# Sliding-window attention feeding a two-layer MLP: memsets and q spreading leave GpSimd, and q of three batches comes in 64-value rows

## The chip, the cores and the metric

The kernel runs on one core of a Trainium2 chip. Its time is device time in microseconds (us) of that core for one execution; lower is better. Before the change it takes 315.79 us, the median of 3 runs (315.48 to 317.68).

## The reference

```python
def _attn_ref(q, k, v):                       # each (8, 8, 576, 64): batch, head, position, dim
    scores = (1.0 / np.sqrt(64)) * np.matmul(q, k.transpose(0, 1, 3, 2))
    rel = pos[:, None] - pos[None, :]
    scores = np.where((rel >= 0) & (rel < 64), scores, -1e9)
    attn = softmax(scores)                    # over the keys
    return np.matmul(attn, v)
x = attn_out.transpose(0, 2, 1, 3).reshape(4608, 512)
h = x @ w_in                                  # 512 -> 2048
out = (h - np.tanh(h)) @ w_out                # 2048 -> 512, float32 (4608, 512)
```

A query sees itself and the 63 keys before it.

## The kernel before, in words

Everything is computed in bfloat16 and added up in float32. Two pieces of work run beside each other: attention of 8 batches, and an MLP over 9 chunks of 512 tokens. A chunk can start when the attention of the batches that its tokens lie in has been normalised and transposed.

**Attention.** A batch has 4 pairs of heads, so that pairs are numbered 0 to 31 (`g`), and 9 windows of 64 queries. For each window the scores of 64 queries of both heads against 128 keys are one matmul (three windows at a time, `Rp`, line 300), the exponential is ScalarE's (`Rx`, line 305), a multiply with a mask is VectorE's (`M`, line 393), and two pairs at a time are multiplied with v (`PP`, line 418) and normalised (`DR`, `DN`, lines 426 to 438). The result is transposed into the chunk's tile by TensorE in the early batches (`Xp`) and by a DMA transpose in the later ones (`Y`, line 472).

**Where v comes from.** v is loaded in rows of 64 values into two tiles `vw` that alternate by batch (`LV`, line 160). Two VectorE copies of 64 partitions by 2080 values then put the other half of each window in place (`Z`, `cross_rows`, lines 166 and 167).

**Where k and q come from.** k of batches 3 to 7 is loaded in rows of 64 values (`lr`, line 176) and turned by a DMA transpose into `kw` (`tk`, line 181). q takes two roads. In batches 3 to 5 (`LQ`, `load_all`, line 114) a batch's q is loaded in runs of 384 values, cast from the loaded tile to a tile of the pair (`cq`, `cast`, line 88 on ScalarE or 90 on VectorE), transposed by TensorE (`Ep`, line 261) and copied from PSUM into `qT` (`Ea`, `Eb`). In batches 6 and 7 GpSimd spreads the two heads of a pair over the halves of a zeroed tile `qz` (`cz`, `cast_q`, line 128, two copies a pair), the tile is written to DRAM (`bo`, line 133) and read back by a DMA transpose into `qT` (`td`, line 138). There are two `qz`, which alternate by pair: a spreading into one waits until the write of two pairs before has left it. The zeros in `qz` (`z`, line 235) and the pads of `kw` (`mk`, line 220) are written once, by GpSimd.

**MLP.** `H` is a tile of the first layer (four matmuls of 512 columns, line 487), `A` its tanh on ScalarE (line 495), `G` the subtraction on VectorE (line 501), `W` four matmuls of the second layer (line 526), and `O` a copy out of PSUM on ScalarE or VectorE with the store on SyncE's DMA queue (line 542).

**Order.** Nothing is scheduled at run time. `PLAN` is a list of words such as `H.3.11` or `cz.25`, written out in full; `play` issues them one after the other, and each engine executes its own instructions in that order. A word with `.a` or `.v` runs on ScalarE or VectorE. Loads (`lk`, `lq`, `LQ`, `LV`, `lr`, `wi`, `wo`) are issued by GpSimd in its own order with its other instructions. Words that issue DMAs from SyncE (`tk`, `bo`, `td`, `Y`, and the store of `O`) stand in SyncE's order.

Of the kernel before, what the change touches and what calls it, by code (L numbers as in the profile page):

```python
# [15 lines left out]
def kernel(  # L16
# [9 lines left out]
    nc = tc.nc  # L26
    B, H, S, D = q.shape
# [58 lines left out]
    def move(eng, o, i):  # L86
        if eng is nc.scalar:
            nc.scalar.activation(o, i, ACT.Copy)  # L88
        else:
            eng.tensor_copy(o, i)  # L90
# [20 lines left out]
    def load_all(b, n):  # L111

        t = rows_all[n][b % 2][0:P]
        nc.gpsimd.dma_start(out=t, in_=(q if n == "q" else k)[b].rearrange("h (p e) d -> p h (e d)", e=E))
        for pr in range(NP):
            stage[b * NP + pr, n] = t[:, pr::NP]
# [7 lines left out]
    def cast_q(g):  # L124

        i = stage.pop((g, "q")).rearrange("p h (e d) -> p h e d", d=D)
        for h in range(2):
            nc.gpsimd.tensor_copy(qz[g % 2][:, h, :, 64 * h:64 * h + 64], i[:, h])  # L128
# [89 lines left out]
    def pads_kw():  # L218
        for i in range(2):
            nc.gpsimd.memset(kw[i][:, :, 0:64], 0.0)  # L220
# [13 lines left out]
    def more_zeros(i):  # L234
        nc.gpsimd.memset(qz[i], 0.0)
# [318 lines left out]
    def subtract(c, m, s=None):  # L554
# [6 lines left out]
        LK=lambda b: load_all(b, "k"), LQ=lambda b: load_all(b, "q"),  # L561
# [14 lines left out]
    def play(script):  # L576
# [5 lines left out]
        mt.0 mv.0 mt.1 lk.3.p lq.0.s lk.1.p u ck.1.a lq.1.p LV.0.1 cq.0.a lk.0.s i mv.1 U.11 cq.1.v mq.1 U.1  # L582
        LV.0.3 Ep.1.3 Fp.1.2 Ec.1.3.v lq.3.p ck.0.v U.4 U.1.3 h Fc.1.2.a LV.0.2 Fp.0.2 LV.0.0 LV.0.4 Rp.1.1.4
        lk.2.p Ep.0.3 Ec.0.3.v lq.2.p Fc.0.2.a Rx.1.1.4 Rp.1.0.0 Rp.0.1.4 Rx.1.0.0 Fp.3.2 Ep.3.3 Rx.0.1.4
        Rp.0.0.0 Fc.3.2.v Z.0 Ec.3.3.a Rx.0.0.0 U.4 lk.5.p lk.7.p lq.5.p lk.6.p n Rp.3.1.4 P.0 Fp.2.2 D.0 Ep.2.3
        Rp.3.0.0 Fc.2.2.a lq.4.p lk.4.p Ec.2.3.v lq.7.p U.2 ck.5.v Rx.3.0.0 P.1 Rx.3.1.4 Fp.5.3 cq.5.v Rp.2.0.0
        Fc.5.3.a Rp.2.1.4 Rx.2.0.0 D.1 Rx.2.1.4 Ep.5.3 Xp.0.0.1.2 lv.1.1.1 P.3 wi.0 Eb.5.3.v wi.1 ck.4.v
        Ea.5.3.a wi.2 Xc.0.0.1.2.a Fp.4.3 Fc.4.3.a Rp.5.0.4 lv.1.1.0 lq.6.p D.3 lt.1 cq.4.v P.2 Rx.5.0.4
        lv.1.0.1 lv.1.0.0 Xp.0.0.0.3 Rp.5.1.4 D.2 Xc.0.0.0.3.a U.1.2 Xp.0.1.0.3 Xp.0.1.1.2 Rx.5.1.4 Xc.0.1.1.2.v
        U.1 mq.0 Rp.5.2.4 Xc.0.1.0.3.a H.0.1 A.0.1 H.0.0 ck.7.v Rx.5.2.4 G.0.1 H.0.2 wo.0 za.1.1.p lq.8.p A.0.0  # L590
        G.0.0 A.0.2 Ep.4.3 H.0.4 Eb.4.3.a wo.1 Ea.4.3.a A.0.4 ck.6.v G.0.2 H.0.3 Fp.7.3 Rp.4.2.4 lk.8.p H.0.5
        A.0.3 N Fc.7.3.v zb.1.0.p Rx.4.2.4 G.0.3 Fp.6.3 A.0.5 zb.1.1.p Rp.4.0.4 Rx.4.0.4 G.0.5 H.0.6 Rp.4.1.4
        G.0.4 A.0.6 Fc.6.3.a G.0.6 wo.2 wo.3 H.0.8 cq.6.v lq.9.p H.0.7 lk.9.p cq.7.v H.0.9 A.0.8 G.0.8 A.0.7
        lv.1.3.0 G.0.7 Ep.7.3 A.0.9 G.0.9 H.0.11 Eb.7.3.a Rx.4.1.4 A.0.11 za.1.0.v lv.1.2.0 Ea.7.3.v lv.1.2.1
        H.0.10 H.0.12 lv.1.3.1 Rp.7.2.4 G.0.11 lr.3.3.0 A.0.10 lk.10.p G.0.10 Ep.6.3 A.0.12 Eb.6.3.a lq.11.p
        Ea.6.3.a G.0.12 H.0.14 A.0.14 H.0.13 LV.2.1 Rx.7.2.4 M.4 H.0.15 lk.11.p Rp.6.0.4 M.5 Rx.6.0.4 PP.4
        G.0.14 A.0.15 lq.10.p zb.1.3.p cq.8.v LQ.3 DR.4 G.0.15 Rp.7.0.4 LV.2.0 Rx.7.0.4 W.0.0.0 Rp.6.2.4 A.0.13
        DN.4.0 W.0.0.1 ck.8.v Ep.8.3 Rx.6.2.4 Rp.6.1.4 Rx.6.1.4 LV.2.3 Ea.8.3.v Eb.8.3.v G.0.13 W.0.1.0 M.6
        W.0.0.2 Rp.7.1.4 W.0.1.1 DN.4.1 Fp.8.3 W.0.1.2 W.0.0.3 LV.2.2 Rx.7.1.4 lr.3.3.1 cq.9.v Fc.8.3.a Rp.8.2.4
        Rx.8.2.4 O.0.0.v Ep.9.3 Ea.9.3.a Eb.9.3.a W.0.1.3 W.0.2.0 O.0.1.a ck.9.v Fp.9.3 M.7 Rp.8.0.4 W.0.2.1  # L600
        Rx.8.0.4 W.0.3.0 DN.4.2 lr.3.2.1 Fc.9.3.a zb.1.2.v Xp.1.0.0.3 za.1.2.v lr.3.4.1 Xc.1.0.0.3.a Rp.9.2.4
        za.1.3.v ck.10.v PP.6 lr.3.1.0 DR.6 Xp.1.0.1.3 DN.6.1 lr.3.4.0 tk.3.3 LV.2.4 DN.6.2 lr.3.1.1 W.0.2.2
        Rx.9.2.4 W.0.2.3 DN.6.0 W.0.3.1 lr.3.2.0 Xc.1.0.1.3.v Xp.1.1.0.3 Xc.1.1.0.3.v Rp.9.1.4 W.0.3.2 ck.11.v
        lr.3.0.1 Xp.1.1.1.3 W.0.3.3 Xc.1.1.1.3.v Rx.9.1.4 Rp.8.1.4 O.0.2.a cq.10.a Ep.10.3 H.1.0 O.0.3.v
        Rx.8.1.4 Rp.9.0.4 H.1.1 A.1.0 Eb.10.3.v A.1.1 H.1.2 cq.11.v Ea.10.3.v Fp.10.3 z G.1.0 Rx.9.0.4 G.1.1
        cq.13.v H.1.3 A.1.2 H.1.4 Fc.10.3.a A.1.3 G.1.2 Rp.10.1.4 A.1.4 M.9 Fp.11.3 cq.12.v H.1.5 lr.3.0.0
        tk.3.4 G.1.3 Rx.10.1.4 Rp.10.2.4 H.1.6 Fc.11.3.a A.1.5 lr.4.4.0 lr.4.3.1 G.1.4 Rx.10.2.4 Ep.11.3 M.8
        Ea.11.3.a Eb.11.3.a G.1.5 mk H.1.7 lr.4.0.1 A.1.6 Rp.10.0.4 H.1.8 Ep.12.3 tk.3.2 LV.3.2 A.1.7 Z.2
        Rx.10.0.4 Ea.12.3.a PP.8 Rp.11.1.4 G.1.6 A.1.8 H.1.9 G.1.7 M.10 G.1.8 Eb.12.3.a A.1.9 lr.5.4.0 Rx.11.1.4
        DR.8 H.1.10 H.1.11 A.1.10 lr.4.1.0 G.1.9 Rp.11.0.4 H.1.12 A.1.11 DN.8.1 G.1.10 Rx.11.0.4 A.1.12 Ep.13.3  # L610
        U.1.2 Rp.11.2.4 lr.4.2.1 H.1.13 DN.8.2 Eb.13.3.a G.1.11 tk.3.1 Rx.11.2.4 DN.8.0 tk.3.0 H.1.14 LV.3.1
        Ea.13.3.a G.1.12 Rp.12.2.4 A.1.13 lr.4.4.1 Rx.12.2.4 Xp.2.0.1.3 M.11 H.1.15 Xc.2.0.1.3.a G.1.13
        Rp.12.1.4 PP.10 DR.10 A.1.14 DN.10.1 Rx.12.1.4 Xp.2.0.0.3 lr.4.2.0 LV.3.3 DN.10.2 W.1.0.0 Xc.2.0.0.3.a
        Rp.13.0.4 A.1.15 LQ.4 W.1.0.1 lr.5.4.1 Rx.13.0.4 DN.10.0 cq.15.a G.1.14 Xp.2.1.1.3 Xc.2.1.1.3.a
        Rp.12.0.4 G.1.15 cq.14.v Rx.12.0.4 W.1.0.2 Xp.2.1.0.3 Xc.2.1.0.3.a W.1.0.3 LV.3.0 lr.4.0.0 M.12 H.2.1
        Ep.14.3 A.2.1 O.1.0.v Rp.13.2.4 Ea.14.3.v W.1.1.0 H.2.0 Rx.13.2.4 tk.4.2 G.2.1 Eb.14.3.a lr.4.1.1 tk.4.0
        Rp.13.1.4 A.2.0 W.1.1.1 G.2.0 W.1.1.2 H.2.3 Rx.13.1.4 Ep.15.3 A.2.3 G.2.3 H.2.2 W.1.1.3 M.13 Ea.15.3.a
# [88 lines left out]
```

## Time and profile before

| | |
|---|---|
| median of 3 runs | 315.79 us |
| the profiled execution | 316.02 us |
| its span, first to last instruction | 314.2 us |
| TensorE matmuls issued (weight loads in the trace) | 2413 |
| mean granted TensorE clock | 0.999 |
| HBM read, written | 36.70 MB, 11.80 MB |

The span is the time from the first to the last instruction in the trace; about 1.8 us of the execution lie outside it. Busy time of TensorE is a union of modelled matmul times, so that a small wait between two matmuls can be hidden in it. POOL is GpSimd, DVE VectorE, ACT ScalarE, PE TensorE with PEld its weight loads, SP SyncE. A DMA queue's share can be above 100%, since packets on one DMA engine overlap.

### The profile page before, as it was taken

The page shows a single profiled execution, that of the slowest core. Times are in us where ns is not written, and L with a number is a line of the kernel's source. Part 1 is how long each engine was busy: PE and PEld are TensorE (multiplying, and loading weights), DVE is VectorE, ACT ScalarE, POOL GpSimd, SP SyncE. Part 2 cuts the span into 40 slices and gives each one's busy share as a digit, 9 for nine tenths or more (in the row PEclk, how much of TensorE's full clock was granted, in tenths as well). Part 3 has the DMA queues.
Part 4 walks back from the last instruction along what each step waited for, and adds up shares of the span by engine and source line. Part 5 has one row for each costly group of instructions (what it writes and reads, how often), then busy time and mean ns, then how long its engine had stood idle before and what let it go on. Part 6 is the DMA issues. An engine that isn't in the chain of part 4 may idle for free.

```text
span 314.2 us, 6083 instructions
## 1 busy us (share of the span) xinstructions
PE 302.0 (96%) x2385; PEld 165.1 (53%) x2413; DVE 188.3 (60%) x323; ACT 171.2 (55%) x320; POOL 111.4 (35%) x164
## 2 busy tenths in 40 slices
PE   6988999998999999999999999999999999999995
PEld 2565555655655556555555545555554444544444
DVE  1685987699857876667655545864674434343400
ACT  3677865488956867657355536444333543433311
POOL 8990655769909460492532540000000000000000
PEclk9999999999999999999999999999999999999999
DMA  9999999999999999997999996581004110010111
GB/s 156 149 169 206 170 203 147 184 102 153 131 147 119 143 184 165 132 133 160 166 167 193 195 202 154 111 179 40 34 35 109 57 45 33 33 37 33 67 69 67
DMA packets 113133, 39.11 MB, mean 124 GB/s; under 512 B 96336, under 2 KB 107600, under 8 KB 113104
## 3 DMA queue, kind: packets, MB, share of 16 engines
q0 software_dynamic: 72064, 18.06, 69.1%
q1 hardware_dynamic: 41040, 20.65, 28.9%
q8 instruction: 19, 0.31, 0.4%
q14 instruction: 10, 0.08, 0.1%
HBM read 36.70 MB, written 11.80 MB: 154 GB/s over the span
## 4 chain that ended last, share of the span: by engine, by line
PE 82%; POOL 6%; DMA 5%; DVE 4%; issue 1%; ACT 1%; POOLq 0%; DVEq 0%; ACTq 0%
PE ps L526 38%; PE ps L487 34%; DMA qall<-in_q_dram 5%; PE ps L300 4%; PE ps L418 3%; DVE gT L501 2%; POOL kall L108 1%; POOL vw L160 1%; PE ps L261 1%; POOL qall L108 1%; PE ps L519 1%; POOL wi L189 1%; PE ps L453 1%; DVE vw L167 1%; DVE qb L90 1%
## 5 line engine op out<-in xcount | busy, mean ns | idle before, releaser
L501 DVE TENSOR_TENSOR gT<-ps,th 128x512 bf16<-128x512 f32 x144 | 97.3, 688 | 80.6 <-ACT th L495 80.0
L487 PE MATMUL ps<-xT,wi 128*128 128x512 bf16 x576 | 141.6, 379 | 0.5 <-DMA wi<-in_moe_w_in_dram 0.3
L526 PE MATMUL ps<-w_out_sb,gT 128*128 128x512 bf16 x532 | 131.8, 379 | 1.4
L495 ACT ACTIVATE th<-ps 128x512 f32<-128x512 f32 x144 | 84.7, 597 | 78.3 <-PE ps L487 74.9
L487 PEld LDWEIGHTS <-wi 128*128 128x128 bf16 x576 | 62.0, 113 | 49.7 <-DMA wi<-in_moe_w_in_dram 0.5
L526 PEld LDWEIGHTS <-gT 128*128 128x128 bf16 x560 | 53.1, 98 | 56.9
L305 ACT ACTIVATE pt<-ps 128x384 bf16<-128x384 f32 (+2 forms) x92 | 45.8, 503 | 20.7 <-PE ps L300 19.5
L176 POOL DMA_DIRECT2D kall<-in_k_dram x50 | 37.1, 758 | 26.5 <-DMA kw<-kall 16.2
L160 POOL DMA_DIRECT2D vw<-in_v_dram x35 | 30.5, 877 | 11.2 <-PE ps L418 8.3
L88 ACT ACTIVATE ysb<-ps 128x512 f32<-128x512 f32 (+1 forms) x23 | 13.3, 578 | 28.4 <-PE ps L526 25.9
L393 DVE TENSOR_TENSOR pt<-pt,ps 128x1152 bf16<-128x1152 bf16 x28 | 20.7, 747 | 2.3 <-ACT pt L305 2.2
L300 PEld LDWEIGHTS <-kw 128*128 128x128 bf16 x180 | 14.4, 98 | 11.7 <-issue 0.4
L88 ACT ACTIVATE qt<-ps 64x576 bf16<-64x576 bf16 x30 | 19.3, 642 | 1.3 <-PE ps L300 0.3
L300 PE MATMUL ps<-qt,kw 128*128 128x128 bf16 x180 | 19.0, 219 | 0.0
L128 POOL COPY qz<-qall 96x384 bf16<-96x384 bf16 x16 | 7.6, 521 | 22.6 <-DMA qd<-qz 12.0
L438 DVE TENSOR_TENSOR xs<-ps,rcp 128x384 bf16<-128x384 f32 x28 | 15.0, 549 | 0.1
L418 PE MATMUL ps<-vw,pt 128*64 128x65 bf16 x504 | 10.7, 197 | 1.5 <-DVE vw L167 1.5
L418 PEld LDWEIGHTS <-pt 128*64 128x64 bf16 x504 | 9.3, 111 | 4.5 <-issue 2.8
L90 DVE COPY ysb<-ps 128x512 f32<-128x512 f32 x14 | 9.6, 686 | 2.6 <-PE ps L526 2.6
L225 PE MATMUL ps<-warm 128*128 128x512 bf16 x26 | 8.9, 478 | 2.2 <-DVE warm L206 2.1
L261 PE MATMUL ps<-ident,qb 96*128 96x96 bf16 x132 | 9.3, 206 | 1.4 <-DVE qb L90 1.4
L261 PEld LDWEIGHTS <-qb 96*128 96x128 bf16 x132 | 7.5, 97 | 4.5 <-DVE qb L90 1.9
(69 smaller groups left out, 169.6 us busy)
## 6 DMA issues: line engine op xcount, KB each, us to landing
out_dram<-ysb SPq DMA_DIRECT2D x35, 256.0 KB, 2.2
vw<-in_v_dram POOLq DMA_DIRECT2D x28, 128.0 KB, 6.0
qall<-in_q_dram POOLq DMA_DIRECT2D x5, 576.0 KB, 8.2
kall<-in_k_dram POOLq DMA_DIRECT2D x40, 64.0 KB, 5.6
qd<-qz SPq DMA_DIRECT2D x8, 288.0 KB, 3.4
w_out_sb<-in_moe_w_out_dram POOLq DMA_DIRECT2D x4, 512.0 KB, 9.2
kall<-in_k_dram POOLq DMA_DIRECT2D x11, 144.0 KB, 5.0
qall<-in_q_dram POOLq DMA_DIRECT2D x11, 144.0 KB, 5.0
```

What stands on the lines that cost most here:

```text
L88: nc.scalar.activation(o, i, ACT.Copy)
L160: nc.gpsimd.dma_start(out=w[:, 2 * i + 1, :, 0:D] if i < NF else w[64:128, 2 * i, :, 0:D], in_=v[b, :, 128 * i:128 * i + n].rearrange("h p ...
L176: nc.gpsimd.dma_start(out=token_rows(b)[0:c, i, :, h, :], in_=k[b, NP * h:NP * h + NP, 128 * i:128 * i + c].rearrange("r p d -> p r d"))
L261: nc.tensor.transpose(tp[:, e, :], src[:, e, :], ident[:P, :P])
L300: nc.tensor.matmul(sp[:, i], kt[:, 64 * j:64 * j + 128], qT[g % NR][:, :, 64 * j:64 * j + 64], start=first, stop=first or i == n - 1)
L305: nc.scalar.activation(PT[g % NPT][:, js[0]:js[0] + len(js), :].rearrange("p i (h t) -> p i h t", h=2), sp, ACT.Exp, scale=scale)
L393: nc.vector.tensor_tensor(p, p, mask.unsqueeze(1).to_broadcast([128, 2 * NJ, 64]), ALU.mult)
L418: nc.tensor.matmul(ps[r, bank, 65 * i:65 * i + 65], PT[(g + r2) % NPT][:, j, r], vw[b % 2][:, j, p0 + r2 + NP * h, :], start=True, stop=True)
L487: nc.tensor.matmul(hp, w_in_tile(ki, m), chunk_tile(c)[:, n.start // 64:n.stop // 64, ki % 2, 64 * (ki // 2):64 * (ki // 2) + 64], start=( ...
L495: nc.scalar.activation(th[:, n], hp, ACT.Tanh)
L501: nc.vector.tensor_tensor(gT[c][:, m, columns(s)], hp, th, ALU.subtract)
L526: nc.tensor.matmul(yp, gT[c][:, m, s * 128:(s + 1) * 128], w_out_sb[:, m, :], start=n == 1 and i == 0, stop=n == 4 and i == 3)
```

## The change

Five things are changed at once.

1. The zeros of both `qz` and the pads of both `kw` are written by VectorE.
2. The spreading of q of batches 6 and 7 (`cz`) is done by ScalarE (pairs 24, 25, 29, 31) and VectorE (26, 27, 28, 30).
3. q of batches 5, 6 and 7 is no longer loaded with one DMA a batch in runs of 384 values but with two (`Lq`), one for heads 0 to 3 and one for heads 4 to 7, in rows of 64 values that land so that the two heads of a pair lie side by side.
4. With that layout TensorE transposes q of batch 5 straight from the loaded tile; the four casts `cq.20` to `cq.23` (two on ScalarE, two on VectorE) are gone.
5. `PLAN` is a new order throughout, and some casts, copies out of PSUM and stores change between ScalarE and VectorE.

```diff
-    def load_all(b, n):
-        t = rows_all[n][b % 2][0:P]
-        nc.gpsimd.dma_start(out=t, in_=(q if n == "q" else k)[b].rearrange("h (p e) d -> p h (e d)", e=E))
+    def load_q_rows(b, half):
+        t = rows_all["q"][b % 2][0:P].rearrange("p h f -> p (h f)").rearrange("p (e r h d) -> p e r h d", e=E, r=NP, h=2)
+        nc.gpsimd.dma_start(out=t[:, :, :, half],
+                            in_=q[b, NP * half:NP * half + NP].rearrange("r (p e) d -> p e r d", e=E))
         for pr in range(NP):
-            stage[b * NP + pr, n] = t[:, pr::NP]
+            rows[b * NP + pr, "q"] = t[:, :, pr]
+
+    def load_q(b):
+        t = rows_all["q"][b % 2][0:P]
+        nc.gpsimd.dma_start(out=t, in_=q[b].rearrange("h (p e) d -> p h (e d)", e=E))
+        for pr in range(NP):
+            stage[b * NP + pr, "q"] = t[:, pr::NP]
...
-    def cast_q(g):
-        i = stage.pop((g, "q")).rearrange("p h (e d) -> p h e d", d=D)
+    def cast_q(g, eng):
+        i = rows.pop((g, "q"))
         for h in range(2):
-            nc.gpsimd.tensor_copy(qz[g % 2][:, h, :, 64 * h:64 * h + 64], i[:, h])
+            move(eng, qz[g % 2][:, h, :, 64 * h:64 * h + 64], i[:, :, h])
...
-            nc.gpsimd.memset(kw[i][:, :, 0:64], 0.0)
+            nc.vector.memset(kw[i][:, :, 0:64], 0.0)
...
-        nc.gpsimd.memset(qz[i], 0.0)
+        nc.vector.memset(qz[i], 0.0)
```

Some stretches of the order, shortened to the words that matter:

```text
before  Fp.10.3 z G.1.0 Rx.9.0.4 G.1.1 ... G.1.5 mk H.1.7 ... Rp.10.0.4 H.1.8 Ep.12.3 ... A.1.7 Z.2 Rx.10.0.4 Ea.12.3.a PP.8
after   Rp.7.0.4 z PP.4 Rx.7.0.4 mk G.0.14 A.0.15 W.0.0.0 ... Z.2 Rp.10.2.4 ... Ep.11.3 ... H.1.6 Rp.10.0.4 ... H.1.7 ... Ep.12.3 G.1.7 H.1.8 PP.8
before  LQ.5 ... cq.21.a ... cq.20.v ... Ep.20.3
after   Lq.5.0 ... Lq.5.1 ... Lq.6.0 ... Ep.20.3 ... Lq.6.1 ... PP.18 G.3.10 cz.25.a
before  Rp.22.0.4 ... H.4.5 W.3.1.0 H.4.6 M.22 PP.22
after   Rp.22.0.4 H.4.4 W.3.0.3 H.4.5 W.3.1.0 H.4.6 H.4.7 W.3.1.1 M.22 H.4.8 PP.22
```

Counted over the whole program, TensorE issues 2413 matmuls in both, 26 of them the warming ones of line 225; VectorE goes from 323 instructions to 337, ScalarE from 319 to 321, GpSimd from 160 to 143 (memsets of constants left out), and SyncE's DMAs stay at 90.

## The prediction

> **What bounds the kernel now.** I read the page first, then the chain of waits, the table of who waited for whom, the timeline around the one long wait of TensorE, and the DMA queues by stretch.
>
> ```profile
> PE 302.0 (96%) x2385; PEld 165.1 (53%) x2413; DVE 188.3 (60%) x323; ACT 171.2 (55%) x320; POOL 111.4 (35%) x164
> DMA  9999999999999999997999996581004110010111
> 176.65 3.45 PE ps L526 x16
> ```
>
> Busy time by engine, DMA by slice, and one link of the chain. TensorE is busy 302.0 of 314.2 us at a granted clock of 0.999, and 82% of the chain is its own. Sixteen matmuls of 512 columns take 3.45 us where nothing interrupts them, so four (one word `H` or `W`) take 0.863. Both kernels issue the same 2413 matmuls, so only time in which TensorE waits can be won. Its idle time is 12.2 us in all: 3.5 in the first 10 us, 1.8 between 20 and 30, 1.5 between 70 and 80, under 0.2 in nearly every other ten.
>
> ```profile
> POOL kall L176 <- DMA kw<-kall: 16.2, 2, 8.7
> POOL qz L128 <- DMA qd<-qz: 12.0, 2, 6.0
> POOL qz L128 <- issue: 5.8, 1, 5.8
> POOL qz L128 <- DMA qall<-in_q_dram: 4.8, 1, 4.8
> PE ps L418 <- DVE vw L167: 1.5, 1, 1.5
> ```
>
> Who waited for whom: us, times, longest. The last line is TensorE's one long wait after the start. GpSimd waits 22.6 us (12.0 + 5.8 + 4.8) at the spreading of q, and every load behind it waits too.
>
> ```profile
> 68.99 3.24 POOL L235 MEMSET qz<- 96x1536 bf16 x2
> 69.53 1.38 DVE L166 COPY vw<-vw 64x2080 bf16<-64x2080 bf16 x1
> 70.92 1.86 DVE L167 COPY vw<-vw 64x2080 bf16<-64x2080 bf16 x1
> 72.83 0.76 PE L418 MATMUL ps<-vw,pt 128*64 128x65 bf16 x36 [1.52 <-DVE vw L167]
> ...
> L166 DVE COPY vw<-vw x7: 697/697/1384, 13.8 to 199.8; 64x2080 bf16<-64x2080 bf16 x7
> L167 DVE COPY vw<-vw x7: 695/696/1857, 14.6 to 200.5; 64x2080 bf16<-64x2080 bf16 x7
> ```
>
> The timeline, and the two copies over the whole run (min/median/max ns). The copies of `Z.2` take twice to nearly three times their median exactly while GpSimd zeroes `qz`, and `PP.8` waits 1.52 us for them.
>
> **Zeros to VectorE.** Both copies at their medians end at 69.53 + 0.70 + 0.70 = 70.93, before TensorE is ready at 71.3. The whole 1.5 us goes. The new order also puts `Ep.11.3`, `H.1.6` to `H.1.8`, `Ep.12.3` and two groups of scores (some 3.8 us) between `Z.2` and `PP.8`, so what is late next has room. VectorE pays for the memsets beside `PP.4`: 128x576 words take 538 ns, so 768 words 0.72 each, and the two pads (128 words, between 85 ns for 32 and 538 for 576) some 0.17 each: 1.8 us, hidden behind `W.0.0.0` and what follows if VectorE catches up.
>
> The Trainium skill (SBUF — State Buffer, Terms) says that VectorE and GpSimd take a shared pair of ports exclusively, and that the loser is blocked for a whole instruction. The trace agrees that they collide, not that one stands still: a copy blocked until the second memset's end at 72.2 could not have ended at 70.91. Held until then the two would have ended at 73.6, and the gain would be 2.3 us instead of 1.5. By that sentence copies beside GpSimd's spreading would be slow as well; none of that size is in the trace there.
>
> **Spreading to ScalarE and VectorE.**
>
> ```profile
> L128 POOL COPY qz<-qall 96x384 bf16<-96x384 bf16 x16 | 7.6, 521 | 22.6 <-DMA qd<-qz 12.0 <-issue 5.8 <-DMA qall<-in_q_dram 4.8
> L90 DVE COPY qb<-qall 96x768 bf16<-96x768 bf16 x15 | 6.3, 426 | 5.3 <-DMA qall<-in_q_dram 5.2
> L88 ACT ACTIVATE qb<-qall 96x768 bf16<-96x768 bf16 x6 | 4.9, 834 | 0.0
> L88 ACT ACTIVATE xT<-ps 128x384 bf16<-128x384 bf16 x2 | 1.0, 492 | 0.0
> ```
>
> GpSimd loses 16 copies (7.6 us) and the 22.6 us of waits ahead of them. ScalarE gets 8 copies of 384 values at 0.49 (the last row): 3.9 us, less `cq.21` and `cq.22` at 0.83: +2.3. VectorE gets 8, each between half of 0.34 and 0.43, say 0.23: 1.8, less two casts at 0.43: +1.0. The swaps between the engines, counted word by word, put about 3.3 more on VectorE and take 2.1 off ScalarE. So VectorE has about 6 more of 188 and ScalarE none; both have room on average, and the four casts are off TensorE's supply.
>
> The waits move as well. A spreading now stands in ScalarE's or VectorE's order with a tanh or a subtraction behind it, and TensorE behind that. Against the write of `qz` two pairs before, the new order leaves at least 10 us of TensorE's work (`bo.24` to `cz.26`, `bo.25` to `cz.27` and so on). Against the load it does not: between `Lq.6.1` and `cz.25.a` stand two `H`, one `W`, two groups of scores and `PP.18`, 3 × 0.86 + 2 × 0.33 + 0.70 = 4.0 us.
>
> **64-value rows.** A batch's q is 768 packets of 384 values now and 4608 of 64 values then: 2304 become 13824 over three batches.
>
> ```profile
> q0 software_dynamic: 72064, 18.06, 69.1%
> ...
> q0 software_dynamic: 3952, 0.49, 64.4%
> ...
> q0 software_dynamic: 25578, 4.59, 128.4%
> ...
> DMA packets 1340, 0.52 MB, mean 174 GB/s; under 512 B 811, under 2 KB 1339, under 8 KB 1339
> ```
>
> The queue of GpSimd's loads: whole run, 148 to 160 us (rows of 64 values alone, 124 B a packet), 85 to 142 us, and all DMA from 130.5 to 133.5 (the load of batch 6's q). A packet's time on its engine is 0.644 × 16 × 12 us / 3952 = 31 ns in the second and 46 ns in the third; packets overlap, and the third stretch passes 25578 / 57 = 449 a us. An old load is 0.59 MB at 174 GB/s, 3.4 us. So the new rows cost 13824 × 31 ns / 16 = 27 us at the least price and 40 at the other, 31 at the measured rate, less 3 × 3.4 = 10: 17 to 29 us more, and I take 20, by the rate, since it counts the overlap. Below nothing is excluded: the bytes are the same. Against it stand the 22.6 us of waits that leave GpSimd's order, so the loads run ahead by about what they cost. Six issues replace three; one takes 0.66 us for 192 packets and 0.88 for 1024, say 1.2 for 2304: +4.8 us on GpSimd, less than the 11.4 of copies and memsets that leave it.
>
> The Trainium skill (DMA: Bandwidth & Descriptors, Specifications) says that a transfer under 512 bytes falls short of line rate and is read, changed and written back. That speaks against this part. The trace agrees that small ones are dear (31 ns for 128 bytes, against 3.4 us × 16 / 768 = 71 ns for 768); taken as doubled writing it would give 3 × 3.4 = 10 us more, under the room.
>
> **The order.** Between the last scores of pairs 22 and 23 and `PP.22` stood `H.4.5`, `W.3.1.0` and `H.4.6` (2.6 us), and weight loads waited 0.4 us for the mask; eight such words (6.9 us) stand there now. Pairs 18 and 19 go from 5.0 to 10.5. I take 0.5 us for these. At the start the first scores still wait for q and k of pair 1; I take 0, within one us either way. For the tight place before `cz.25` I add 0.3.
>
> **Sum.** 316.0 (the profiled execution) − 1.5 − 0.5 + 0.3 = 314.3; the median of the runs is 0.2 below that execution, so **314.2 us**.
>
> **Rivals.**
>
> *The loads come late (slower).* TensorE's order holds `Ep.20.3`, which now reads the loaded tile, and the scores of batch 7, behind loads that pass about 20 us more; ScalarE holds `cz.25`. `Lq.5.1` has some 9 us of TensorE's work before `Ep.20.3`. For it: DMA is at 9 tenths until 188 us, and even now keys of the last batch are turned at 194.4 with the first scores on them at 199.0. Against it: the 22.6 us. It decides from the point where the new rows cost more than 22.6 plus about 2 of slack: (24.6 + 10.2) × 16 / 13824 = 40 ns a packet, between my two rows. At 46 ns they cost 29, so 29 − 24.6 = 4.7 us late with the gain of 1.7 kept, 319.0; with a second such wait at `cz.25`, 319.5. Chance 0.27.
>
> *VectorE gives it back.* From 60 to 80 us it is busy 9.0 and 9.9 of each 10 us; 1.8 us of memsets and the swaps before it can bring a wait for `G` where `Z.2` was: 1.5 lost again, 316.0. Against it: `Z.2` itself shrinks by 1.85. Chance 0.16.
>
> *More is won.* With GpSimd silent, the idle 1.8 us of TensorE between 20 and 30 us goes too, since the first weights of the MLP are issued two loads sooner and `H.0.1` waited for them: 314.2 − 1.8 = 312.4. Against it: that stretch also waits for copies out of PSUM. Chance 0.16.
>
> **How the numbers follow.** Forecast (313 to 315.5) 0.41, the rivals 0.27, 0.16 and 0.16. A measurement of this kernel can tell about 1% from no change, 3.2 us: under 312.6 or over 318.9. Faster by that: most of the third rival and little of the forecast, 0.18. Slower: two thirds of the first and some unknown wait, 0.22. The rest is 0.60. The range leaves a tenth on each side: 311.9 to 319.5.
>
> **What would show it.** Right: the copies of `vw` at 0.70 throughout and no wait of `PP.8` for them; GpSimd with nothing but DMA issues after 60 us; TensorE's idle time some 2 us lower. The rows: 83,600 packets in GpSimd's queue, its share of 16 engines 5 to 9 points higher. Wrong: `Ep.20.3`, or scores of batch 7, waiting for DMA; tanh waiting behind `cz`; VectorE's `Z` waiting for v; a first matmul later than 8.4 us.

## The result, and the profile after

The kernel is slower: 319.50 us, the median of 6 runs (318.09 to 323.13), against 315.63 before; the ratio is 1.0105, 95% interval 1.0064 to 1.0146. Disturbed runs, that of 323.13 and three of g1's below with its profiled execution among them, are in no ratio. Measured three more times it was 1.0063 (1.0035 to 1.0091), 1.0157 (1.0125 to 1.0189) and 1.0063 (1.0038 to 1.0089). So 2 to 5 us are lost. The profiled execution took 319.36 us with a span of 317.7, against 316.02 and 314.2.

Every ratio below is against the kernel before, run in the same group, that is at the same sitting: e1 to e4, e5 to e8, the f, the g and the h kernels. After itself was run again in the groups f, g and h alone. Since its own ratio moves by almost one per cent between groups, the times of e1 to e8 place a kernel against before, but tell differences of under one per cent from after only roughly; there the traces have to speak.

The page of after, busy time and the queue of GpSimd's loads:

```profile
PE 303.7 (96%) x2413; PEld 165.2 (52%) x2413; DVE 192.1 (60%) x337; ACT 172.3 (54%) x322; POOL 108.8 (34%) x147
...
q0 software_dynamic: 83632, 18.06, 73.4%
```

The sums are near the forecast: VectorE gained 3.8 us (forecast about 6), ScalarE 1.1 (forecast none), and the queue went from 69.1% to 73.4% with 11568 packets more. None of them says where 3.5 us went. The table of who waited for whom does (us, times, longest), of TensorE:

```profile
PE ps L495 <- DVE gT L509: 3.0, 2, 2.8
...
PE ps L308 <- DMA qt<-qd: 1.4, 1, 1.4
...
PE ps L534 <- DVE gT L509: 0.5, 1, 0.5
```

and of GpSimd:

```profile
POOL qall L114 <- PE ps L269: 16.0, 1, 16.0
POOL kall L184 <- DMA kw<-kall: 14.0, 2, 8.1
POOL vw L168 <- PE ps L426: 10.9, 1, 10.9
```

The wait of `PP.8` for `vw` is gone. New are a wait of 2.8 for `G`, one of 1.4 for DMA at line 308, and GpSimd's 16.0 us at the load `Lq.7.1`. Its wait at `LV.7.0`, the first load of the last batch's v, is not new. The table of waits of before has it, at 8.3 us and for the same `PP.22`:

```profile
POOL vw L160 <- PE ps L418: 8.3, 1, 8.3
```

What is new there is the number of loads that stand behind it in GpSimd's order.

To place the loss, the lag of TensorE behind the kernel before was read off the traces: the start of a word less the time at which the kernel before had issued the same amount of work (words that only one of them has issued by then count with their usual length, 0.33 us for a group of scores, 0.86 for an `H` or `W`). It is good to some 0.2 us. The table is in us, for four profiled executions of after (f3, g3 and h3 are after once more) and for two kernels told of below; "before at" is the time in the kernel before.

```text
word       before at  after    f3    g3    h3  |   h1    e8
H.0.8         33.0     -1.1   0.1  -0.6  -1.0  | -0.8  -0.7
H.0.10        36.9      2.1   1.7   0.4  -0.2  |  0.9   1.7
Rp.7.1        47.2      2.4   2.2   0.9   0.1  |  1.2   2.0
PP.8          71.2      2.7   2.8   1.6   0.8  |  1.5   2.2
H.1.12        76.4      1.1   1.2   0.0  -0.8  | -0.1   0.6
Ep.19.3      116.7      1.3   1.5   0.4  -0.6  | -0.1   0.8
W.2.0.3      119.8      1.5   1.8   2.3   1.1  |  1.2   2.4
W.2.2.1      138.1      1.5   1.8   3.5   1.1  |  1.7   2.4
W.3.0.1      152.7      1.8   2.0   3.7   1.4  |  1.8   2.1
H.5.3        184.0      1.9   2.2   3.9   1.6  |  2.0   2.2
H.5.9        196.2      3.5   2.9   4.6   2.6  |  2.6   3.9
W.8.3.3      309.6      3.5   2.9   4.7   2.6  |  2.6   3.9
```

After runs ahead until 33 us in three of the four, since the MLP's weights come two loads sooner (the first landed at 24.3 us instead of 25.5). It loses 0.8 to 3.2 us at `H.0.9`, in three of four more than it had won. At `PP.8` each of the four wins the 1.6 us of `Z.2`. It loses again near 118 us in two of four (1.7 and 1.9), 1.2 near 137 in g3 alone, where the scores `Rp.20` wait for keys, 0.25 near 150, and 0.7 to 1.5 near 185. After 196 us nothing changes. The mean of the four at the end is 3.4 us.

**At 34 us.** The timeline of after (start, us, engine, line, operation, out<-in, count, the idle time before and what ended it):

```profile
32.86 1.57 ACT L503 ACTIVATE th<-ps 128x512 f32<-128x512 f32 x3 [0.49 <-PE ps L495]
...
36.14 0.36 DVE L90 COPY qb<-qall 96x768 bf16<-96x768 bf16 x1 [1.90 <-DMA qall<-in_q_dram]
...
36.41 1.88 DVE L509 TENSOR_TENSOR gT<-ps,th 128x512 bf16<-128x512 f32 x3
37.15 1.02 PE L495 MATMUL ps<-xT,wi 128*128 128x512 bf16 x4 [2.82 <-DVE gT L509]
```

The tanh of `G.0.6` is done at 33.5. `G.0.6` starts at 36.41, since the cast `cq.7.v` stands ahead of it on VectorE and waits for a load. Before, that cast stood behind `G.0.6`, and its load was issued at 16.1 and landed at 21.1; now the load goes behind the three `w_in` loads and lands at 36.05. `H.0.9` needs the PSUM bank that `G.0.6` reads. The four executions bear this out: the later the load lands, the larger the loss at `H.0.9`, from 0.8 us at a landing of 33.7 (h3) over 1.0 at 34.2 (g3) and 1.6 at 35.5 (f3) to 3.2 at 36.05.

**At 185 us.** SyncE's transposes `td.27` and the next one, and the weight load of the scores `Rp.27.1.4`, which need `td.27`, in the timeline of after:

```profile
178.40 7.45 SPq L146 DMA_TRANSPOSE qt<-qd  x2
...
188.57 0.17 PEld L308 LDWEIGHTS <-kw 128*128 128x128 bf16 x3 [1.85 <-DMA qt<-qd]
```

`td.27`, the first of the two transposes, is issued at 178.4 and lands at 188.5, 10.1 us later. Before, it was the second of the two in this row of the timeline, was issued at 182.5 and landed at 186.3, 3.8 us later:

```profile
181.19 3.18 SPq L138 DMA_TRANSPOSE qt<-qd  x2
```

In after GpSimd had been held until 166.3 by `LV.7.0` (10.9 us, for `PP.22`), and then issued 16 loads in 15 us. Before, 10 loads were issued between 162 and 181 us, six of them by 167.

### The profile page after: what moved, and what is told of

Same layout as the page of the kernel before. It is cut to its first block, busy times and chain, and to the rows that moved or that the text cites. A ratio compares the mean times of both kernels' runs of the same rounds, so it can differ in the third digit from the quotient of the medians.

```text
span 317.7 us, 6099 instructions
## 1 busy us (share of the span) xinstructions
PE 303.7 (96%) x2413; PEld 165.2 (52%) x2413; DVE 192.1 (60%) x337; ACT 172.3 (54%) x322; POOL 108.8 (34%) x147
## 3 DMA queue, kind: packets, MB, share of 16 engines
q0 software_dynamic: 83632, 18.06, 73.4%
## 4 chain that ended last, share of the span: by engine, by line
PE 65%; DMA 17%; POOL 10%; issue 3%; DVE 3%; ACT 2%; POOLq 0%; DVEq 0%; ACTq 0%
PE ps L534 31%; PE ps L495 27%; DMA qall<-in_q_dram 5%; DMA vw<-in_v_dram 4%; DMA qt<-qd 3%; PE ps L308 3%; POOL vw L168 3%; DMA kall<-in_k_dram 3%; PE ps L426 2%; POOL kall L184 2%; DMA kw<-kall 2%; POOL qall L108 1%; POOL kall L108 1%; PE ps L527 1%; PE ps L269 1%
## 5 line engine op out<-in xcount | busy, mean ns | idle before, releaser
L534 PE MATMUL ps<-w_out_sb,gT 128*128 128x512 bf16 x560 | 136.4, 379 | 0.5 <-DVE gT L509 0.5
L313 ACT ACTIVATE pt<-ps 128x384 bf16<-128x384 f32 (+1 forms) x92 | 45.8, 504 | 26.1 <-PE ps L308 18.8
L184 POOL DMA_DIRECT2D kall<-in_k_dram x50 | 41.5, 977 | 24.6 <-DMA kw<-kall 14.0
L168 POOL DMA_DIRECT2D vw<-in_v_dram x35 | 33.4, 977 | 13.6 <-PE ps L426 10.9
L88 ACT ACTIVATE ysb<-ps 128x512 f32<-128x512 f32 (+1 forms) x21 | 12.1, 577 | 17.7 <-PE ps L534 15.1
L401 DVE TENSOR_TENSOR pt<-pt,ps 128x1152 bf16<-128x1152 bf16 x28 | 20.7, 743 | 0.1
L88 ACT ACTIVATE qt<-ps 64x576 bf16<-64x576 bf16 x28 | 18.0, 642 | 3.5 <-PE ps L269 2.2
L114 POOL DMA_DIRECT2D qall<-in_q_dram x6 | 10.2, 1706 | 16.4 <-PE ps L269 16.0
L90 DVE COPY ysb<-ps 128x512 f32<-128x512 f32 x16 | 10.9, 682 | 4.0 <-PE ps L534 4.0
L90 DVE COPY qt<-ps 64x576 bf16<-64x576 bf16 x12 | 9.0, 750 | 6.0 <-ACT qt L88 2.9
L108 POOL DMA_DIRECT2D qall<-in_q_dram x11 | 7.4, 670 | 5.9 <-PE ps L308 2.2
```

Of the source, the lines that this page charges most:

```text
L168: nc.gpsimd.dma_start(out=w[:, 2 * i + 1, :, 0:D] if i < NF else w[64:128, 2 * i, :, 0:D], in_=v[b, :, 128 * i:128 * i + n].rearrange("h p ...
L184: nc.gpsimd.dma_start(out=token_rows(b)[0:c, i, :, h, :], in_=k[b, NP * h:NP * h + NP, 128 * i:128 * i + c].rearrange("r p d -> p r d"))
L313: nc.scalar.activation(PT[g % NPT][:, js[0]:js[0] + len(js), :].rearrange("p i (h t) -> p i h t", h=2), sp, ACT.Exp, scale=scale)
L401: nc.vector.tensor_tensor(p, p, mask.unsqueeze(1).to_broadcast([128, 2 * NJ, 64]), ALU.mult)
L534: nc.tensor.matmul(yp, gT[c][:, m, s * 128:(s + 1) * 128], w_out_sb[:, m, :], start=n == 1 and i == 0, stop=n == 4 and i == 3)
```

## The experiments

Two theories. By the **order** theory the loss is the new `PLAN`: a cast ahead of a subtraction, memsets ahead of another, and waits in GpSimd's queue that hold back loads and then release them together. By the **rows** theory it is the 64-value rows, which take more packets for the same bytes.

### The wait in H.0.9 (e1, e2, g1)

e1 moves words of VectorE and TensorE only:

```diff
- U.1 cq.7.v lv.1.3.0 G.0.6 ... H.0.9 Ep.7.3 G.0.8 G.0.7 ... H.0.11 H.0.10 A.0.9
+ U.1 lv.1.3.0 G.0.6 ... H.0.9 G.0.8 G.0.7 cq.7.v ... H.0.11 H.0.10 Ep.7.3 A.0.9
```

> After, with one cast of VectorE (cq.7.v, q of pair 7) moved behind the subtractions G.0.6 to G.0.7, and TensorE's transposes of that tile (Ep.7.3) moved behind H.0.10; no load moves. Order theory: the 2.96 us wait of TensorE in H.0.9 comes from G.0.6 standing behind a cast whose load lands at 36.05; it goes whole, since H.0.11 and H.0.10 cover the landing, and the time falls by 2.5 to 2.9 us, to about 316.7. Rival (late loads): the loads of this stretch are late for whatever stands next; the wait comes back at Ep.7.3 or at the first second-layer matmuls, and less than 1 us is won (318.5 to 319.4).

318.71 us, 1.0104 (1.0056 to 1.0153) against before: the 2.5 us that the order theory expected are not won. `H.0.9` starts at 33.94 without a wait, and at `H.0.10` the kernel is still ahead of before (lag −0.8, after's is 2.1). But in this execution the load had landed at 33.62, so the cast would have held little in its old place too; that it holds `G.0.6` rests on after's trace and on the landings above. Then TensorE is idle for 1.4 us ahead of `Ep.6.3`, behind a copy of ScalarE, and at `H.0.12` the lag is 0.7 to 0.9. By `PP.4` part of it is given back.

e2 moves one load:

```diff
- lk.6.p ... wi.0 ... wi.1 ... wi.2 ... lq.8.p lv.1.1.1 ... lq.7.p
+ lk.6.p ... lq.7.p wi.0 ... wi.1 ... wi.2 ... lq.8.p lv.1.1.1
```

> After, with the load of q of pair 7 (lq.7.p) issued ahead of the three w_in loads, as before the change; nothing else moves. Order theory: the load lands before 23 us and the wait in H.0.9 goes; the w_in loads land 0.5 to 1 us later, which the first H may pay for: 316.7 to 317.5. Rival (late loads): the wait only changes its place, to the w_in tiles: 318.5 to 319.4.

317.42 us, 1.0060 (1.0032 to 1.0089). In its profiled execution (318.97, near the slow end of its 12 runs) `lq.7` lands at 22.7, but `wi.0` at 26.3 instead of 24.3 and `H.0.1` starts 1.9 later: the lag at `H.0.10` is 2.1, after's. The first theory's 2.8 us is not won whole by either.

g1 puts `lq.7.p` directly behind `wi.2`, `lq.8.p` behind `lq.6.p`, and `cq.8.v` ahead of `Ea.6.3.v`.

> After, with the load of pair 7's q (lq.7.p) directly behind the last w_in load, the load of pair 8's (lq.8.p) behind lq.6.p, and the cast cq.8.v that needs it moved on VectorE from ahead of ck.6 to ahead of Ea.6.3; nothing else moves. By the order theory the load of pair 7 lands before 33.5 us, cq.7.v is done when G.0.6's tanh is, the step at Ep.7.3 (0.1 to 3.0 us, mean 1.3, in six executions) is under 0.4 in this one, and the time is 1 to 1.3 us below after in the same group. Rival (the whole stage is bound by what DMA moves): the wait goes to Ep.6.3, Ep.7.3 or the first second-layer matmuls and the time is after's.

318.98 us, 1.0090 (1.0061 to 1.0119), beside after's 1.0157 in the same group, some 2 us less, which is more than was expected. The trace shows less: the step at `Ep.7.3` is 0.3, as foretold, but about 0.9 comes back by 41 us. So the places exist, and in these three traces a good part of what one frees waits at the next; how much a better start is worth stays open.

### The burst after 166 us (e3, e4, e8)

```diff
e3
- LV.7.0 ... Lq.7.0 ... LV.6.0 lr.7.4.0 ... LV.6.4 ... lr.7.1.0 ... lr.7.1.1 ... lr.7.3.0 ... lr.7.0.1
+ Lq.7.0 LV.6.0 lr.7.4.0 LV.6.4 lr.7.1.0 lr.7.1.1 lr.7.3.0 lr.7.0.1 LV.7.0
e4 (load_q_rows, batches 6 and 7 only)
+ a = rows_all["q"][b % 2][0:P]
+ nc.gpsimd.dma_start(out=a[:, NP * half:NP * half + NP],
+                     in_=q[b, NP * half:NP * half + NP].rearrange("r (p e) d -> p r (e d)", e=E))
e8 (load_q_rows, heads 4 to 7 of batch 7)
+ own = qk_pool.tile([P, 2, E * D], F32, tag="f", name="qown")   # a buffer that nothing else uses
```

> After, with eight loads of GpSimd's queue (Lq.7.0, LV.6.0, lr.7.4.0, LV.6.4, lr.7.1.0, lr.7.1.1, lr.7.3.0, lr.7.0.1) moved ahead of LV.7.0, which waits 10.9 us for PP.22; nothing else moves. Order theory: they leave before 165 us, the queue is thinner when td.27 is issued, td.27 lands within 5 us instead of 10.1, and the 1.91 us wait of Rp.27.1.4 goes: 317.4 to 317.8. Rival (64-value rows): the volume is the same and only moves; td.24, tk.6 and td.25 are late instead and the time stays at 319 or rises.

318.56 us, 1.0093 (1.0060 to 1.0125). `td.27` lands 4.3 us after its issue and `Rp.27.1.4` does not wait: the loads behind `LV.7.0` are what delays it. But the rival's sentence holds too, for `Rp.24.0.4` waits at 167 us instead, for keys (`tk.6`). The timeline of e3:

```profile
167.56 0.17 PEld L308 LDWEIGHTS <-kw 128*128 128x128 bf16 x3 [1.47 <-DMA kw<-kall]
```

In these runs loads that leave together delay the transposes that are then on their way, `td.27` in after and `tk.6` in e3.

> After, with q of batches 6 and 7 loaded in runs of 384 values into the old layout (batch 5 as after); words and order are the same, the spreading reads with another stride. GpSimd's queue has 4 x 1920 = 7680 packets fewer, about 75,950. Rows theory: the queue is thinner wherever batch 7's q passes, td.27 lands within 5 us, Z.5 takes 1.4 us instead of 2.4 and the time falls by 1.5 to 2.5 us. Order theory: the eleven other loads behind LV.7.0 are the burst, td.27 still takes over 7 us to land, and less than 1 us is won (318.4 to 319.4). The 2.96 us wait in H.0.9 stays in both.

319.68 us, 1.0115 (1.0069 to 1.0160), with 75952 packets. `td.27` takes 10.4 us to land with 3840 packets fewer in batch 7. The rows are not what delays it. The step at `Rp.27.1.4` is 1.3. One thing did follow the packets: the copies of `Z.5` took 1.80 us, where after has 2.43 (the rows theory expected 1.4).

> After, with heads 4 to 7 of batch 7's q landing in a tile of their own, so that Lq.7.1 does not wait for TensorE's Ep.23.3; same words and order. GpSimd's 16.0 us wait goes and the five to eight loads behind it are issued 15 to 20 us sooner. If that wait is what makes td.27 late, Rp.27.1.4 no longer waits and the time falls by 1.5 to 2 us (317.5 to 318). If it is LV.7.0's wait for PP.22 with Lq.7.0, LV.6.0 and lr.7 behind it, those still leave after 166 us, the 1.6 to 1.9 us wait stays, and less than 0.8 us is won.

320.22 us, 1.0142 (1.0105 to 1.0179). The 16.0 us wait is gone and `Lq.7.1` leaves at 132.9, yet `td.27` lands 10.2 us after its issue and the wait stays, 1.7 us, as the second half of the expectation has it. GpSimd only waits longer at the next place. The table of e8, whose longest wait is that of `LV.7.0`, 20.7 us instead of 10.9:

```profile
POOL vw L176 <- PE ps L434: 26.6, 2, 20.7
```

`LV.7.0` and the loads behind it leave at 166.6, as in after. Another thing was won that no theory had named. The timeline around `Z.5`, of after and then of e8:

```profile
147.89 1.62 POOL L114 DMA_DIRECT2D qall<-in_q_dram  x1 [16.05 <-PE ps L269]
149.07 2.68 POOL L168 DMA_DIRECT2D vw<-in_v_dram  x2
...
149.84 1.48 DVE L174 COPY vw<-vw 64x2080 bf16<-64x2080 bf16 x1
...
150.81 3.83 POOL L184 DMA_DIRECT2D kall<-in_k_dram  x4
...
151.33 0.95 DVE L175 COPY vw<-vw 64x2080 bf16<-64x2080 bf16 x1
```

```profile
150.72 0.70 DVE L182 COPY vw<-vw 64x2080 bf16<-64x2080 bf16 x1
...
151.43 0.69 DVE L183 COPY vw<-vw 64x2080 bf16<-64x2080 bf16 x1
```

The copies take 2.43 us while GpSimd issues the loads that its long wait held back, and 1.39 where it issues none. `M.21` and `PP.20` stand behind them: the lag from `Rp.23.0.4` to `W.3.0.1` grows by 0.5 in after and falls by 0.1 in e8.

### What the memsets cost VectorE (e5, f1, f2)

e5 is before with `nc.vector.memset` for `qz` and `kw`; the words stay where they were.

> Before, with the zeros of qz and the pads of kw written by VectorE at the same places of the order; nothing else changes. If the step on the zeros is right, the copies of Z.2 take 0.70 us each, PP.8 does not wait 1.52 us, and the time falls by 1.2 to 1.5 us, to 314.2 to 314.6. Rival (VectorE gives it back): the memsets, 1.8 us on VectorE, make G.1.0 and what follows late: 315.5 to 316.

316.40 us, 1.0046 (1.0028 to 1.0064): a little slower, and the rival is right. The timeline of e5:

```profile
64.40 1.50 DVE L235 MEMSET qz<- 96x768 uint32 x2
...
66.51 1.89 PE L487 MATMUL ps<-xT,wi 128*128 128x512 bf16 x8 [1.46 <-DVE gT L501]
...
73.42 0.76 PE L418 MATMUL ps<-vw,pt 128*64 128x65 bf16 x36 [0.30 <-DVE vw L167]
```

`PP.8` wins 1.2, and `H.1.4` has paid 1.5 for it seven microseconds earlier. The lag of e5 at the end is 0.6 us, 0.35 of it from the first 35 us; the rest of the 1.3 us between the medians is not in this trace.

f1 leaves the memsets on GpSimd and moves `z` ahead of `lr.3.4.0`.

> Before, with GpSimd's two memsets of qz some 5 us earlier in its order (ahead of lr.3.4.0, where GpSimd was idle 3.6 us); they stay on GpSimd. If Z.2 was slow only because the memsets ran beside it, its two copies take 0.70 us each, PP.8's 1.52 us wait goes at no price on VectorE, and the time falls by 1.2 to 1.6 us below the kernel before. Rival: any price for the memsets is paid by whatever VectorE does beside them (casts cq.11, cq.13 and G.1.0), 0.5 to 1 us of wait at H.1.3 to H.1.5, and less than 0.7 us is won.

315.66 us, 1.0003 (0.9978 to 1.0028). The rival again. The timeline of f1:

```profile
62.14 2.69 POOL L235 MEMSET qz<- 96x1536 bf16 x2
...
63.99 1.05 DVE L90 COPY qb<-qall 96x768 bf16<-96x768 bf16 x1
```

The cast `cq.11` took 0.35 before. It pays 0.7 for the memset beside it, with `G.1.0` behind it, and the lag of f1 grows by 0.7 there before it falls by 1.25 at `PP.8`.

f2 is after with `z` moved ahead of `Ea.9.3.v` and `mk` ahead of `DR.6`, into gaps of VectorE.

> After, with VectorE's memsets moved to gaps of its own: qz ahead of Ea.9.3 and the pads of kw ahead of DR.6, where VectorE waited 1.3 to 1.7 us. If the memsets ahead of G.0.14 cost TensorE time, the step of 0.8 to 0.9 us at W.0.0.0, which six of six profiled executions of after and its variants show, shrinks by 0.5 us or more and nothing new waits: 0.5 to 0.8 us less than after. Rival (the step is the new order's, not the memsets'): the step stays, and the time is after's.

319.01 us, 1.0086 (1.0056 to 1.0115), against 1.0063 (1.0035 to 1.0091) for after in the same group: the times do not tell them apart. The trace does: the step from `Rp.7.0.4` to `Rp.6.2.4` is 0.28 instead of 0.82 and nothing waits at the new places. So the memsets cost 0.5 us in after's order.

### All places together (e6, f4, g2)

e6 is e1, e2 and e3 in one.

> After, with the moves of the first three runs together: cq.7.v behind G.0.7 and Ep.7.3 behind H.0.10, lq.7.p ahead of the w_in loads, and eight loads ahead of LV.7.0. Order theory: the waits in H.0.9 and of Rp.27.1.4 are both gone and the time is 315.5 to 316.5, level with before. Rival (64-value rows, or ScalarE and VectorE loaded with the spreading): the time stays above 317.5, with new waits of TensorE for DMA, tanh or G spread over the run.

320.94 us, 1.0193 (1.0167 to 1.0219), the slowest of all. `Rp.24.0.4` starts 2.9 us late behind the loads that e3 moved. Two more steps of 0.7 follow, and they are not waits: from 170.8 to 174.3 us the granted clock of TensorE is 0.50, and its matmuls start 0.43 us apart instead of 0.22. After's wait of 2.8 us at 34 us has no such stretch behind it (clock 1.00). The order theory's number failed: places that are mended one at a time do not add up.

f4 has f2's memsets and e8's own tile, `lq.7.p` ahead of `wi.2`, and seven loads ahead of `LV.7.0`. With the 16 us wait gone, `Lq.7.1` leaves at 131.4 and the seven between 145.6 and 151.4.

> After, with four places mended: the memsets in VectorE's gaps (as in the second run of this group), lq.7.p ahead of the last w_in load, heads 4 to 7 of batch 7's q in a tile of their own, and seven loads (LV.6.0, LV.6.4, lr.7.4.0, lr.7.1.0, lr.7.1.1, lr.7.3.0, lr.7.0.1) ahead of LV.7.0, so that they leave in the 130s and 140s. If the loss is these places, 315.5 to 317 and no wait of Rp.24.0.4 or Rp.27.1.4 over 0.5 us; if the loads only collide elsewhere, H.3.0, Rp.24.0.4 or tk.6 waits 1 to 3 us and the time stays at 318 or above.

315.81 us, 1.0013 (0.9987 to 1.0039), against 1.0063 for after in the same group: level with before. In its profiled execution (317.87, the second slowest of 12) `td.27` lands in 6.5 us and the step at `Rp.27.1.4` is 0.0; 2.3 us are lost between `W.2.0.3` and `W.2.2.1` instead, where `Rp.20` waits for keys: the transposes `tk.5` land 8 to 10 us after their issue, beside `Lq.7.1` and the loads of batch 5's v.

g2 is f4 with g1's start.

> After, with all places mended: the start as in the first run of this group, the memsets in VectorE's gaps, heads 4 to 7 of batch 7's q in a tile of their own, and the seven loads ahead of LV.7.0. If the loss is these places and no other, 314.5 to 315.5, 0 to 1 us below the kernel before, since the wait of PP.8 stays away. If loads that leave 15 us sooner collide with tk.5, Y.3 or td.24, 316 or above, with a wait of H.3.0, H.3.9 or Rp.24.0.4 over 1 us.

317.11 us, 1.0058 (1.0027 to 1.0090), against 1.0157 for after in the same group. The second half came true: `H.3.9` and its neighbours lose 2.0 us. Beside after in their own groups the mended versions are 0.5% (f4), 0.7% (g1) and 1.0% (g2) below it, so part of the loss is in these places. No version beat the kernel before.

### After once more (f3, g3)

> After, unchanged, once more: how much do its waits differ between executions? By the order theory the wait in H.0.9 depends on when the load of pair 7 lands among saturated DMA (33.6 to 36.1 us seen) and lies between 0 and 3 us; the steps at W.0.0.0 (0.8 to 0.9), Z.5 to PP.20 (0.8 to 0.9) and td.27 (1.2 to 1.7) are there again, since they hang on the order. Median 318.5 to 320.

> After, unchanged, a third time, as the base of this group: 317 to 320 by both theories, 0.5 to 1.2% above the kernel before; the steps at W.0.0.0, PP.20 and Rp.27.1.4 again, the wait in H.0.9 anywhere between 0 and 3 us.

317.44 us, 1.0063 (1.0035 to 1.0091), and 320.62, 1.0157 (1.0125 to 1.0189). The table in the first section has their lags. The load of pair 7 landed at 35.5 and 34.2. In g3, `H.3.0` waits for the transposes of `Y.3`, which after and f3 do not. Its timeline:

```profile
120.13 0.58 PEld L495 LDWEIGHTS <-wi 128*128 128x128 bf16 x4 [1.93 <-DMA xT<-xs]
```

The traces of after and its variants fall in two groups here. Where SyncE issued `Y.3` 3.3 us or more behind GpSimd's `Lq.5.1` (after, e1, e2, e3, f2, f3), it landed 3.7 to 5.6 us after its issue; where 2.3 us or less behind it, or ahead of it (e4, e6, e8, f4, g2, g3, h1, h3), 6.0 to 8.6 us. h1, which has no 64-value rows of q, is among the slow ones with 8.1. So an execution that is ahead of time at this point seems to lose its lead here. That is a pattern of 14 traces, and no run moved the load.

### Order or rows (e7, h1, h2, h3)

e7 and h2 are one kernel: before's order and engines, q of batches 5 to 7 in 64-value rows, batch 5 uncast. h1 is after's order and engines with all three batches in runs of 384 values; it has 24 small transposes more, some 0.4 us. h3 is after. "Order" here means changes 1, 2 and 5 together: the zeros, the spreading and the words.

```diff
e7, h2 (PLAN of before)
- LQ.5 ... LQ.6 ... LQ.7, cq.21.a cq.20.v cq.22.a cq.23.v
+ Lq.5.0 Lq.5.1 ... Lq.6.0 Lq.6.1 ... Lq.7.0 Lq.7.1
h1 (load_q_rows, all batches as e4)
+ if b == 5: stage[b * NP + pr, "q"] = a[:, pr::NP]
```

> Before, in its own order, with q of batches 5 to 7 loaded in 64-value rows, two DMAs a batch at the places of the one, batch 5 transposed straight from the loaded tile and its four casts left out; zeros and spreading stay on GpSimd. Rows theory: the rows alone make the kernel slower by 1 to 3 us (317 to 319), with waits for q, td or tk after 100 us. Order theory: old room hides them as it hid the casts: 315.2 to 316.2. The queue of GpSimd then has about 83,600 packets, as after.

> After's order and engines, with q of batches 5, 6 and 7 all loaded in runs of 384 values (two DMAs a batch); batch 5 is transposed straight from the loaded tile in twelve pieces of 64 columns a pair instead of six of 128, some 0.1 us a pair more. GpSimd's queue has about 72,100 packets, as before. Order theory: the loss is after's, 0.6 to 1.6% above the kernel before, level with the third run of this group within 0.4%. Rows theory: the rows are the loss, and this one is 1 to 3 us faster than after, 315.5 to 317.5.

> Before, in its own order, with q of batches 5 to 7 in 64-value rows and batch 5 uncast (the kernel of e7_before_rows once more). Order theory: 0 to 0.4% above the kernel before, at least 0.4% below after in this group. Rows theory: 0.6% or more above the kernel before, level with after.

> After, unchanged, as the fourth corner of the square of old and new order by runs of 384 and rows of 64: 317 to 320.6, 0.6 to 1.6% above the kernel before, by both theories.

e7 alone did not settle it: 316.71 us, 1.0044 (1.0013 to 1.0075), its 12 runs spread from 314.77 to 320.41, its profiled execution level with before (span 314.1). The last three ran in one group:

```text
                     runs of 384              rows of 64
old order     1 (before, 315.91 us)   0.9989 (0.9960 to 1.0018)  h2
new order     1.0110 (1.0071 to 1.0149)  h1   1.0063 (1.0038 to 1.0089)  h3
```

The rows cost little in the old order: e7 and h2, the same kernel, are 0.44% above and 0.11% below before, together about 0.15%, and 0.4% at most is left for them. Leaving them out wins nothing in the new. The packets bear the test out: 83632 in h2, 72112 in h1. The new order, with the engines that came with it, is the loss, with 72112 packets as with 83632. TensorE's waits for DMA point the same way. The tables of waits of h2 (of the matmuls; its weight loads have no row for DMA), then of h1 (of the weight loads):

```profile
PE ps L308 <- DMA qt<-qd: 0.4, 1, 0.4
```

```profile
PEld L498 <- DMA xT<-xs: 1.4, 1, 1.4
...
PEld L311 <- DMA qt<-qd: 1.0, 1, 1.0
```

The table of waits of h1 also has GpSimd's 17.9 and 11.8 us, at the same two words:

```profile
POOL qall L114 <- PE ps L268: 17.9, 1, 17.9
POOL vw L171 <- PE ps L429: 11.8, 1, 11.8
```

h2, whose batch 5 is uncast too, has no long wait at `Lq.7.1`: the held tile costs GpSimd time only where the new order asks for it sooner.

## Why the prediction was wrong

It forecast 314.2 us with 0.60 on no change and 0.22 on slower; 319.5 was the end of its range.

The step that failed is the one on GpSimd's loads: 22.6 us of waits leave its order, so "the loads run ahead by about what they cost", and the start costs nothing. The sum has no term for loads that are held in that queue by other waits and then leave together beside SyncE's transposes, nor for a cast that now waits for a load behind 2 MB of weights. The runs showed in their place, as means of four executions: 1.0 us lost at the start, 1.0 at `td.27`, which lands 10.1 us after its issue instead of 3.8, 0.9 near 118 us (1.7 and 1.9 in two of four, its cause argued), and 0.5 for the memsets that were to be hidden. Some 1.6 us more went in smaller steps, and the 1.6 us of `Z.2` were won as forecast: 3.4 us of loss in all where 1.7 of gain were forecast.

By parts:

- *Zeros, −1.5.* The wait of `PP.8` goes: 1.6 us in each of four executions, as forecast (the copies of `vw` are not at 0.70 throughout, though: `Z.5` took 2.43). The reading that no copy stood still does not come out of the trace. The row of 3.24 us is two memsets, the first of which ends at 70.36 and the second at 72.23, and the two copies end at 70.91 and 72.78, each 0.55 us after one of them. In e7 and h2 the second memset ends at 71.37 and 71.39 and the first copy at 71.92 and 71.94, again 0.55. That fits copies that stood still until a memset was over; the 73.6 was worked out from one memset of the whole length. That VectorE's memsets are "hidden behind `W.0.0.0`" failed: 0.5 us, by f2. The memsets' own length was right (0.70 and 0.17 each, forecast 0.72 and 0.17). The same gain was fully paid back in before's order, on VectorE (e5) and half of it on GpSimd (f1). The rival "VectorE gives it back" named the mechanism, and its price of 1.5 is what e5 shows.
- *Spreading, no cost.* ScalarE's copies took 0.51 and VectorE's 0.25 (forecast 0.49 and 0.23), and the lag of after does not grow where pairs 24 and 25 are spread (138 to 141 us) nor where 26 and 27 are (156 to 158). A kernel with the spreading back on GpSimd was not tried, so that it costs nothing is argued.
- *"Against it stand the 22.6 us of waits that leave GpSimd's order, so the loads run ahead."* **This is the step that failed.** The waits for `qz` left; a new one of 16.0 us came at `Lq.7.1`, and that at `LV.7.0` grew from 8.3 to 10.9. The first could be read off the change: uncast, batch 5's tile is held until TensorE's `Ep.23.3` instead of until the casts, and `Lq.7.1` writes it. The second has 16 loads behind it in the new order. GpSimd's last load did leave sooner, at 180.1 us instead of 186.1, but it landed later, at 191.1 instead of 189.3, and the loads that left together held up `td.27`. e8 shows that the 16.0 us alone are not the price: without them the loads wait at `LV.7.0`. e3, with eight loads moved, brings `td.27` back to 4.3 us.
- *64-value rows, 20 us of DMA.* The queue's packet time grew by 0.734 × 317.7 − 0.691 × 314.2 = 16 us per engine, near the 20 taken; the share rose 4.3 points (forecast 5 to 9). An issue of 2304 packets delays GpSimd's next by 1.18 us, as the 1.2 forecast. At most 0.4% of the time is theirs (e7, h2), and h1 wins nothing without them. The rival "the loads come late" had the sign and nearly the time (319.0 to 319.5), but by luck, for it had neither the cause nor the places: `Ep.20.3` and `cz.25` did not wait (`Lq.5.1` landed 11 us ahead of the one, `Lq.6.1` 11 ahead of the other). The 9 and 4.0 us of TensorE's words between load and use were no measure of it: GpSimd issued the two 16.7 and 22 us ahead. What came late were SyncE's transposes (`td.27`, `Y.3`), and the count of packets was not why.
- *The start, 0 within one us.* A gain of up to 1.1 us until `H.0.8` and a loss of 0.8 to 3.2 at `H.0.9` make the lag −0.2 to 2.1 at `H.0.10`, mean 1.0. The prediction asked of a moved spreading what stands behind it on its engine, and did not ask it of the casts, whose loads had moved behind 2 MB of weights.
- *The order, −0.5 and +0.3.* Neither: `PP.22` waits 0.41 us as before, `cz.25` for nothing.
- *The sum.* 314.3 less 0.2 is 314.1, not 314.2.

What adds up in the four executions, by the mean lags of the table (us): 1.0 by `H.0.10`, 0.4 to `Rp.7.1` (the memsets' 0.5 within it), −1.0 to `H.1.12` (the 1.6 of `Z.2` less 0.6 along the way), 1.3 to `W.2.0.3`, 0.3 to `W.2.2.1`, 0.4 to `H.5.3`, 1.0 to `H.5.9`: 3.4.

Shown: changes 1, 2 and 5 together are the cause and the rows are not; `cq.7` holds `G.0.6`; the loads behind `LV.7.0` hold `td.27`; VectorE's memsets cost 0.5 us. Not settled: how much of the 1.0 us at the start a better order could win, since three attempts each met a new wait; what the spreading adds by itself; and why `H.3.0` waits for `Y.3` in g3, h3, h1, e4 and e8 and not in after and f3. That it is the loads issued between 108 and 116 us fits the pattern told above, and wasn't tried.

## What to carry to other kernels

When a wait leaves an in-order queue, look for the next one in that queue before counting the time as won; here the waits for a write of `qz` went, and one came for a tile whose reader had changed from a cast to TensorE. A load that moves behind large ones makes every instruction that reads it a possible stop for what stands behind on that engine, a subtraction that frees PSUM above all. And put a layout change and a new order into separate kernels: the square of the two, run side by side in one group, said which of them mattered where single runs had not.

## What the runs showed of the hardware

- DMA transposes were slow beside GpSimd's loads that left together: `td.27` took 9.6 to 10.7 us from issue to landing in four executions of after, 4.3 with eight loads moved away (e3), 3.8 before. With q in runs of 384 values it took 10.1 too (h1), so it isn't the small packets of q. Its successor's issue alone held SyncE for 5.98 us. The Trainium skill (DMA: Bandwidth & Descriptors, SWDGE vs HWDGE vs iDMA) says that each DMA engine takes turns between queues that software and hardware descriptors feed; the runs agree in that transposes are delayed and not stopped, and show its size.
- VectorE's copies also slow down beside GpSimd's DMA issues, not only beside its memsets: 2.43 us for `Z.5` while loads are issued, 1.39 without. Of the 280 copies of 64 by 2080 values in the 20 traces, 94 took over 0.75 us, and each of these had an instruction of GpSimd beside it; the 120 without one all took 0.70. The other 66 beside one took 0.70 to 0.73, so not every such instruction costs. The Trainium skill (the same page and section) says that GpSimd writes its descriptors into SBUF and names VectorE as the one that locks it out; here VectorE lost too.
- One program differs from execution to execution in when its DMA lands: the load of pair 7, issued within 0.4 us of the same time, landed between 33.7 and 36.1 us in four executions of after.
- After a wait of 3.0 us TensorE was granted half its clock for 3.5 us in one trace (e6, 0.50 from 170.8 to 174.3 us, near 1.00 elsewhere). After's wait of 2.8 us at 34 us was not followed by it. What decides is not shown.
